# One TensorE order, two build-time plans: what a matmul is charged, and a new table by slot

## The chip, the cores and the metric

The kernel runs on one core of one Trainium2 chip. The metric is the device time of one launch in microseconds (us). Three runs of the kernel before gave 1040.53, 1040.58 and 1040.61 us; the median is 1040.58 us.

## The reference

Two attention branches, A and B, read the same `x` (2048 tokens by 640) with their own weights; a sigmoid gate by token mixes their outputs. Each branch has 32 heads of width 20, and works through the tokens in 4 segments of 512:

```python
for s in range(N):                       # 4 segments, for each branch
    qs, ks, vs = q[:, :, s], k[:, :, s], v[:, :, s]
    logits = einsum("bhqd,bhkd->bhqk", qs, ks) * scale + mask     # causal within the segment
    a_dot = einsum("bhqk,bhkd->bhqd", softmax(logits), vs)
    num = einsum("bhld,bhde->bhle", phi(qs), M); den = phi(qs) . z + 1e-6
    outs.append(g * num / den + (1 - g) * a_dot)                  # g by head
    M, z = M + phi(ks)^T vs, z + sum(phi(ks))
o = outs @ wo
result = gate * o_A + (1 - gate) * o_B
```

## The kernel before, in words

The work is cut into 8 blocks (branch and segment), and each block into 8 quads of four heads: 64 quads, and 66 **slots** `i` in which they are worked through. For each quad there are S units (the logits with queries on partitions, whose row maxima VectorE takes, line 1058), one transpose of the maxima (`mrow_unit`, line 1096), T units (the logits again with keys on partitions, the maxima in two extra rows; ScalarE's exp at line 1153 and GpSimd's causal select at line 1154 make `p`), and a PV unit (`pv_unit`, line 1181: 16 fp32 matmuls with 128 rows and 32 columns each, 32 rows in the profile, since an fp32 matmul runs in two passes). Around these lie the products with wq, wk, wv, wo, each split into three terms of hi and lo parts (`product`, line 640, 512 or 320 columns wide), the reads and updates of the memory `M` (`mem_unit`, line 749, and `update_unit`, line 827, fp32 in two passes), and transposes (`turn`, line 787).

Almost every matmul uses 64 of the 128 rows of TensorE: an instruction goes to the lower or to the upper **half**, and one of each half can run side by side. PV, the first two products (line 685) and the last (line 1000) use all rows, so both halves must come to an end before them.

The order of the instructions on every engine is made **while the kernel is built**, by a planner written in the kernel itself. It keeps a clock `now`, a time `lane[half]` at which each half of TensorE is free, and a queue for each other engine with a pace for each of its instructions (`put("D", 0.63, ...)`: VectorE for 0.63 us; A is ScalarE, G GpSimd, S the DMA queue), and `DONE`, the delay until another engine sees the end. `step` picks the half that is free first, and `lane_step` takes for it, in this order, an S or T matmul, the second half of a unit whose first half is done (`seconds`), or the first half of a new unit (`firsts`). What is emitted stands in TensorE's program in this order, and TensorE takes its matmuls in the order of the program. The chip sees only the order and the semaphores: the planner's paces and clocks aren't in the program.

`RULES` is a table by slot: the order of the ten S and T units, and five numbers (`span`, `calm`, `lag`, `room`, `hold`) that say how the slot is spread over the products, when work for VectorE is held back, how long after the first half the second may follow, how many buffers must be free, and by how much the slot begins early. A slot without an entry keeps the entry of the slot before.

The charges of TensorE's instructions before:

```python
STEP, STEPV = 0.2335, 0.1475                      # a product of 512, of 320 columns
(w * 0.000458, ...)                               # S and T, w columns
(0.063, ...)                                      # a transpose
max(0.22, (c - a) * E1 * 0.0017)                  # a memory read;   update: nh * E1 * 0.0017
now[0] = max(now[0], lane[0], lane[1]) + 0.09     # PV; then w * 0.00174 for each kb, and 0.063
```

Of the kernel before, what the change touches and what calls it, by code (L numbers as in the profile page):

```python
# [16 lines left out]
ALU = mybir.AluOpType  # L17

P = 128
# [23 lines left out]
def tile_gated_mix_infini_attn(  # L43
# [47 lines left out]
        0: "STSTSTSTST 1.010 2.38 0.36 8 0.0",  # L91
        1: "TSTSTSTSTS 1.010 2.19 0.30 8 0.0",
        3: "TSTSTSTSTS 1.010 2.38 0.30 8 0.0",
        4: "TSTSTSTSTS 1.010 2.38 0.32 6 0.0",
        5: "TTSSTTSSTS 1.010 2.38 0.30 8 0.0",
        6: "TSTSTSTSTS 1.010 2.38 0.30 8 0.0",
        8: "TSTSTSTSTS 1.045 2.38 0.30 4 0.0",
        9: "TSTSTSTSTS 1.010 2.38 0.35 8 0.0",
        10: "TSTSTSTSTS 1.021 2.38 0.32 8 0.0",
        12: "TSTSTSTSTS 1.010 2.38 0.30 8 0.0",  # L100
        14: "TSTSTSTSTS 0.957 2.38 0.37 6 0.0",
        15: "TSTSTSTSTS 0.932 2.30 0.32 8 0.0",
        16: "TSTSTSTSTS 1.010 2.38 0.30 8 0.0",
        19: "TSTSTSTSTS 1.002 2.63 0.30 8 0.0",
        21: "TSTSTSTSTS 1.010 2.51 0.30 4 0.0",
        22: "TSTSTSTSTS 0.927 1.90 0.30 4 0.0",
        23: "TTSTSTSTSS 1.012 2.26 0.37 8 0.0",
        24: "TSTSTSTSTS 1.010 2.38 0.30 8 0.0",
        25: "TSTSTSTSTS 1.010 3.35 0.30 8 0.0",
        27: "TSTSTSTSTS 1.010 2.38 0.30 8 0.0",  # L110
        28: "TSTSTSTSTS 0.939 3.03 0.35 8 0.0",
        30: "TSTSTSTSTS 1.010 2.38 0.30 8 0.0",
        32: "TTSTSTSTSS 1.010 2.38 0.30 8 0.0",
        34: "TSTSTSTSTS 1.010 2.38 0.30 8 0.0",
        36: "TSTSTSTSTS 1.040 2.50 0.30 6 0.0",
        37: "TSTSTSTSTS 0.950 2.38 0.30 6 0.0",
        39: "TSSTTSSTTS 1.010 1.60 0.37 8 0.0",
        41: "TSSTTSSTTS 1.010 2.38 0.33 6 0.0",
        42: "TSTSTSTSTS 0.939 2.38 0.30 4 0.0",
        46: "TSTSTSTSTS 1.010 2.38 0.30 8 0.0",  # L120
        49: "TSTSTSTSTS 1.010 2.38 0.25 4 0.0",
        50: "TSTSTSTSTS 1.010 2.38 0.30 8 0.0",
        54: "TSSTTSSTTS 1.019 3.32 0.30 6 0.0",
        57: "TSTSTSTSTS 1.010 2.38 0.30 8 0.0",
        58: "TSTSTSTSTS 1.014 3.04 0.30 8 0.0",
        60: "TSTSTSTSTS 1.010 2.38 0.30 8 0.0",
        61: "STSTSTSTST 1.047 2.95 0.38 8 6.0",
        62: "TSTSTSTSTS 1.010 2.38 0.30 8 0.0",
        63: "TSTSTSTSTS 1.014 2.38 0.25 4 0.0",
        64: "TSTSTSTSTS 1.010 2.38 0.30 8 0.0",  # L130
    }
    rule = {}
    DONE = {"A": 0.165, "D": 0.11, "G": 0.1, "S": 0.0}
# [69 lines left out]

    def whole(dur, emit):
        now[0] = max(now[0], lane[0], lane[1]) + dur
        got = emit()
        lane[:] = [now[0], now[0]]
        advance(now[0])
        return got
# [160 lines left out]
    STEP, STEPV = 0.2335, 0.1475  # L370

# [47 lines left out]
    def stage(i):  # L419
# [8 lines left out]
        lo_cost = 0.9 if i < 4 else 1.6  # L428
        if kind == "v":
# [6 lines left out]
            def piece(w, a, b, wh, wl, done):  # L436
                n = b - a
                w3 = w.rearrange("p (k n) -> p k n", n=VN)[:, :n, :]

                def landed():  # L440
                    put("A", 0.33 * n, lambda: nc.scalar.copy(wh[:, a:b, :], w3), split_lo, prio=6)

                def split_lo():
                    put("G", 0.8 * n, lambda: nc.gpsimd.tensor_tensor(
                        out=wl[:, a:b, :], in0=w3, in1=r32(wh[:, a:b, :]), op=ALU.subtract), end, prio=4)
# [10 lines left out]
        def got(w):  # L456
# [8 lines left out]
            def split_hi(pair):  # L465
                wh, wl = pair
                put("A", 0.66, lambda: nc.scalar.copy(wh, w3), lambda: put(  # L467
# [15 lines left out]
    def want_x(s, k):  # L483

        def got(hi, lo, st):
            def landed():
                put("A", 0.56, lambda: nc.scalar.copy(hi, r32(st)), low, prio=6)

            def low():
                e, eng, cost = ("D", nc.vector, 0.7) if s == 0 else ("G", nc.gpsimd, 1.3)  # L490
# [91 lines left out]
    def hi_lo_phi(pp, hi, lo, y, dst, m, then, got_phi):  # L582
# [7 lines left out]
        if load["D"] < load["A"]:  # L590
            def over():
                put("D", 0.63, lambda: nc.vector.tensor_scalar(pp, pp, 0.0, 1.0, op0=ALU.max, op1=ALU.add), lambda: put(  # L592
                    "D", 0.63, lambda: nc.vector.tensor_tensor(out=r32(y), in0=pp, in1=r32(y), op=ALU.min), end, prio=1), prio=1)  # L593
# [3 lines left out]
            put("A", 0.49, lambda: nc.scalar.activation(r32(y), pp, AF.Exp), read, prio=1)  # L597
        else:
            both = then_all(2, lambda: put("D", 0.63, lambda: nc.vector.scalar_tensor_tensor(
                out=r32(y), in0=pp, scalar=0.0, in1=r32(y), op0=ALU.max, op1=ALU.add), end, prio=1))  # L600
            hi_lo_out(pp, hi, lo, dst, m, both, then)
            put("A", 0.49, lambda: nc.scalar.activation(r32(y), pp, AF.Relu, scale=-1.0), lambda: put(  # L602
                "A", 0.56, lambda: nc.scalar.activation(r32(y), r32(y), AF.Exp, scale=-1.0), both, prio=1), prio=1)

    def hi_lo_out(src, hi, lo, dst, m, read, then):
        is_q = any(dst is x for x in qd)

        def low():
            put("D", 0.63, lambda: nc.vector.tensor_tensor(out=lo, in0=src, in1=r32(hi), op=ALU.subtract), out, prio=1)  # L609
# [15 lines left out]
        put("A", 0.49, lambda: nc.scalar.copy(hi, src), low, prio=1)  # L625
# [11 lines left out]
    def product(bank_of, terms, step, done):  # L637
        def mm(half, n, start, stop):
# [3 lines left out]
        ops = [[(step, lambda a, z, half=half, n=n: mm(half, n, a, z)) for n in range(len(terms))] for half in range(2)]  # L642
# [86 lines left out]
    def mem_unit(t, n, h):  # L729
# [17 lines left out]
        def mm(half, j, start, stop):  # L747
# [8 lines left out]
        ops = [[(max(0.22, (c - a) * E1 * 0.0017), lambda z0, z1, half=half, j=j: mm(half, j, z0, z1)) for j, (m, a, c) in enumerate(pieces[half])]  # L756
# [24 lines left out]
        return split_unit(*ops, lambda: (read(), put("D", 1.05, weigh, end, prio=4)))  # L781

    def turn(px, block):
# [5 lines left out]
        return [[(0.063, lambda a, z, half=half, n=n: one(half, n)) for n in range(NB)] for half in range(2)]  # L789
# [4 lines left out]
    def back_unit(t, m, pk):  # L794
# [3 lines left out]
        def got(pkn):  # L798
# [4 lines left out]
            either(0.52, lambda: nc.scalar.copy(r32(pkn), b), 0.63, lambda: nc.vector.tensor_copy(r32(pkn), b), end, 3)  # L803
# [16 lines left out]
    def update_unit(t, m, pkn):  # L820
# [5 lines left out]
        def mm(half, n, start, stop):  # L826
# [6 lines left out]
        ops = [[(nh * E1 * 0.0017, lambda a, z, half=half, n=n: mm(half, n, a, z)) for n in range(NB)] for half in range(2)]  # L833
# [5 lines left out]
        def take():  # L839
            big.give(pkn)  # L840
            if s == 0:
                put("D", 0.3, lambda: nc.vector.tensor_copy(mbd[m], v), lambda: (
                    bank.give(b), put("G", 0.8, lambda: keep_own_heads(mbd[m], m), end, prio=2)), prio=3)
            else:
                def got(tmp):
                    def add():
# [3 lines left out]
                    put("D", 0.3, lambda: nc.vector.tensor_copy(tmp[:, :nh, :], v), lambda: (  # L850
                        bank.give(b), put("G", 1.4, add, lambda: (mt_store.give(tmp), end()), prio=2)), prio=3)
# [5 lines left out]
    def job_v(t, half):  # L857
# [9 lines left out]
        for n in range(NB):  # L867
# [7 lines left out]
            def take(pp=pp, n=n):  # L875
                through()
                put("A", 0.37, lambda: nc.scalar.copy(
# [10 lines left out]
    def job_o(t, m):  # L888
# [32 lines left out]
        def got(ot):  # L921
# [8 lines left out]
            def take():  # L930
                if b == 0:
                    put("A", 0.49, lambda: nc.scalar.copy(r32(ot), pp), send, prio=2)  # L932
                elif pt:
                    put("D", 0.63, lambda: nc.vector.tensor_tensor(
# [10 lines left out]
    def job_early(t, m):  # L945
# [21 lines left out]
        def take():  # L967
# [3 lines left out]
            put("D", 0.63, lambda: nc.vector.tensor_tensor(  # L971
# [4 lines left out]
    def job_last(t):  # L976
# [4 lines left out]
        def finish(m):  # L981
# [3 lines left out]
            put("D", 0.63, lambda: nc.vector.tensor_tensor(  # L985
# [54 lines left out]
    def s_unit(i, n):  # L1040
# [5 lines left out]
        for half in range(2):  # L1046
# [3 lines left out]
            def look(half=half, sc=sc):  # L1050
# [5 lines left out]
                def one(pair, qb, off, then):  # L1056
                    w = P * (qb + 1)
                    put("D", w / 960.0 + 0.112, lambda: nc.vector.tensor_tensor_reduce(  # L1058
# [10 lines left out]
            for j, (pair, qb, off) in enumerate(todo):  # L1069
                w = P * (qb + 1)  # L1070
                lane_ops[half].append((w * 0.000458, lambda pair=pair, qb=qb, off=off, w=w, r=r, sc=sc: nc.tensor.matmul(  # L1071
# [5 lines left out]
    def m_unit(i):  # L1077
# [4 lines left out]
        put("A", 0.2, lambda: nc.scalar.copy(mt[:, :, 0, :], m), lambda: put(  # L1082
            "G", 0.25, lambda: nc.gpsimd.tensor_tensor(
# [7 lines left out]
    def mrow_unit(i):  # L1091
# [4 lines left out]
        ops = [[(0.063, lambda a, z, r=r: nc.tensor.transpose(b[:32, r], mtf[r], ident[r, r]))] for r in ROWS]  # L1096

        def got(mr):
# [14 lines left out]
            put("A", 0.26, lambda: nc.scalar.copy(mr, b[:32, :P]), send, prio=1)  # L1113
# [16 lines left out]
    def t_unit(i, n):  # L1130
# [10 lines left out]
        for half in range(2):  # L1141
# [6 lines left out]
            def take(half=half, sc=sc, pt=pt, blocks=blocks):  # L1148
                def finished():
# [3 lines left out]
                put("A", 0.49, lambda: nc.scalar.activation(pt, sc, AF.Exp, scale=SCALE), lambda: (bank.give(sc), put(  # L1153
                    "G", 0.08 + 0.16 * len(todo), lambda: nc.gpsimd.affine_select(  # L1154
# [4 lines left out]
            for j, (pair, kb, off) in enumerate(todo):  # L1159
                w = L - P * kb  # L1160
                lane_ops[half].append((w * 0.000458, lambda pair=pair, kb=kb, off=off, w=w, r=r, sc=sc: nc.tensor.matmul(  # L1161
# [7 lines left out]
    def pv_unit(i):  # L1169
# [3 lines left out]
        now[0] = max(now[0], lane[0], lane[1]) + 0.09  # L1173
        advance(now[0])
        for kb in range(NB):
# [24 lines left out]
        def got(oT):  # L1200
# [5 lines left out]
            either(0.52, lambda: nc.scalar.copy(r32(oT), po), 0.63, lambda: nc.vector.tensor_copy(r32(oT), po), end, 2)  # L1206
# [17 lines left out]
    def fin_unit(i):  # L1224
# [24 lines left out]
        def take():  # L1249
            big.give(oT)  # L1250
            if s == 0:
                put("D", 0.95, lambda: weigh(o), lambda: (bank.give(b), end()), prio=2)
            else:
                def got(tmp):
                    e, eng, cost = ("D", nc.vector, 0.45) if i >= 62 else ("G", nc.gpsimd, 0.9)
                    put("D", 0.95, lambda: weigh(tmp), lambda: (bank.give(b), put(
# [9 lines left out]
    def o_transpose(t, k):  # L1266
# [3 lines left out]
        def got(hi, lo):  # L1270
# [4 lines left out]
            put("A", 0.49, lambda: nc.scalar.copy(hi, b), lambda: put("D", 0.63, lambda: nc.vector.tensor_tensor(  # L1275
# [69 lines left out]
    def lane_step(half):  # L1345
# [7 lines left out]
        if u and max(now[0], lane[half]) >= u["at"]:  # L1353
# [51 lines left out]
    def wait(what):  # L1405
# [6 lines left out]
        now[0] = max(now[0], clk[0])  # L1412
# [124 lines left out]
```

## Time and profile before

| what | value |
|---|---|
| median of three runs | 1040.58 us |
| profiled execution: span on the core | 1038.6 us, 31967 instructions |
| its own time beside the span | only the span is given for this execution; the median lies 2.0 us above it |
| TensorE busy / its weight loads | 1031.3 us (99%) / 874.8 us (84%) |
| VectorE, ScalarE, GpSimd busy | 765.4 us (74%), 661.7 us (64%), 581.7 us (56%) |
| DMA queue q1 | 205.93 MB, 65.7% of 16 engines |

"Busy" counts a matmul from its start to its modelled end, and matmuls overlap: a 512-wide one stands at 404 ns in the table of groups, while a half takes one in a good half of that. So 99% doesn't say that TensorE couldn't be quicker; the distance from one start to the next does. In the timeline a row "x10" is ten like instructions with nothing else between them on the engine, with the start of the first and the time to the end of the last.

### The profile page before, as it was taken

How to read it: one execution, taken by the hardware profiler on the slowest of the kernel's cores; microseconds unless marked ns; L12 is line 12 of the kernel's file. 1: busy time of each engine (PE TensorE's matmuls, PEld its weight loads, DVE VectorE, ACT ScalarE, POOL GpSimd, SP SyncE). 2: the span in 40 equal slices, each digit the busy share in tenths (PEclk: the TensorE clock that was granted, in tenths of full speed). 3: DMA queues.
4: the chain of work that ended last, by engine and by line, in shares of the span. 5: the costliest groups of instructions: out<-in, count | busy, mean ns of one | idle time of the engine just before them, and what ended most of it. 6: DMA issues, size and time to landing. Idle time of an engine off the chain costs nothing.

```text
span 1038.6 us, 31967 instructions
## 1 busy us (share of the span) xinstructions
PE 1031.3 (99%) x11780; PEld 874.8 (84%) x11780; DVE 765.4 (74%) x2726; ACT 661.7 (64%) x1336; POOL 581.7 (56%) x1043
## 2 busy tenths in 40 slices
PE   9999999999999999999999999999999999999998
PEld 7988888898888879898888978989879888888876
DVE  4687787579686788676886868865787867778764
ACT  6367666578565585666756567665676656657681
POOL 4465555566454564666645557555674537636471
PEclk9999999999999999999999999999999999999999
DMA  8996767478466686755855568675585865847531
GB/s 275 290 290 201 224 195 230 132 225 271 143 194 187 181 272 175 241 150 158 261 171 190 172 176 290 194 211 174 161 253 157 266 167 181 273 125 244 140 120 51
DMA packets 110028, 207.97 MB, mean 200 GB/s; under 512 B 12464, under 2 KB 16560, under 8 KB 109872
## 3 DMA queue, kind: packets, MB, share of 16 engines
q1 hardware_dynamic: 109872, 205.93, 65.7%
q8 instruction: 93, 1.52, 0.6%
q14 instruction: 63, 0.52, 0.2%
HBM read 131.43 MB, written 73.40 MB: 197 GB/s over the span
## 4 chain that ended last, share of the span: by engine, by line
PE 92%; DVE 1%; ACT 0%; issue 0%; ACTq 0%; DVEq 0%
PE bank L640 53%; PE bank L1181 14%; PE bank L1071 7%; PE bank L1161 7%; PE bank L787 4%; PE bank L749 3%; PE bank L827 3%; PE bank L1096 1%; PE bank L1000 0%; DVE row L985 0%; ACT p L1153 0%; DVE bank L1058 0%; DVE row L593 0%; ACT row L932 0%; DVE bank L592 0%
## 5 line engine op out<-in xcount | busy, mean ns | idle before, releaser
L1058 DVE CUSTOM_DVE_ANT_0 bank<-bank,tri 128x128 f32<-128x128 f32 (+3 forms) x1024 | 475.1, 518 | 157.4 <-PE bank L1071 126.0
L640 PE MATMUL bank<-row,wh 64*128 64x512 f32 x2308 | 525.7, 404 | 0.0
L1153 ACT ACTIVATE p<-bank 128x512 f32<-128x512 f32 x592 | 326.5, 599 | 141.6 <-PE bank L1161 112.8
L1154 POOL TENSOR_SCALAR_AFFINE_SELECT p<-p 128x256 f32<-128x256 f32 (+1 forms) x592 | 213.9, 369 | 268.5 <-ACT p L1153 252.1
L640 PEld LDWEIGHTS bank<-row,wh 64*128 64x128 f32 x2308 | 326.1, 185 | 11.8 <-issue 1.8
L640 PE MATMUL bank<-row,wl 64*128 64x512 f32 x1154 | 310.3, 402 | 0.0
L469 POOL TENSOR_TENSOR wl<-wst,wh 128x640 fp32r<-128x640 f32 x115 | 179.6, 1565 | 72.0 <-ACT wh L467 71.5
L640 PE MATMUL bank<-wvh,row 64*128 64x320 f32 x1280 | 189.8, 316 | 0.0
L640 PEld LDWEIGHTS bank<-row,wl 64*128 64x128 f32 x1154 | 175.0, 185 | 5.6 <-issue 0.6
L1161 PE MATMUL bank<-qst,kst 62*128 62x128 f32 (+3 forms) x1024 | 173.5, 319 | 0.0
L1071 PE MATMUL bank<-kst,qst 60*128 60x128 f32 (+3 forms) x1024 | 171.7, 320 | 0.2
L640 PEld LDWEIGHTS bank<-wvh,row 64*128 64x128 f32 x1280 | 154.1, 185 | 3.9 <-issue 2.0
L1181 PE MATMUL bank<-p,vst 128*32 128x384 f32 (+3 forms) x1932 | 146.0, 430 | 0.0
L1058 DVE DVE_READ_ACCUMULATOR2_ANT mx<- 128x1 f32 x1024 | 143.3, 140 | 0.0
L1071 PEld LDWEIGHTS bank<-kst,qst 60*128 60x128 f32 x1024 | 123.7, 185 | 12.0 <-issue 2.5
L1161 PEld LDWEIGHTS bank<-qst,kst 62*128 62x128 f32 x1024 | 124.9, 185 | 7.5 <-issue 1.2
L1181 PEld LDWEIGHTS bank<-p,vst 128*32 128x32 f32 x1932 | 58.3, 109 | 85.7 <-issue 61.4
L640 PE MATMUL bank<-wvl,row 64*128 64x320 f32 x640 | 109.4, 312 | 0.0
L467 ACT CAST wh<-wst 128x640 fp32r<-128x640 f32 x119 | 86.2, 735 | 30.8 <-PE bank L640 15.5
L640 PEld LDWEIGHTS bank<-wvl,row 64*128 64x128 f32 x640 | 85.0, 185 | 0.5 <-issue 0.2
L609 DVE TENSOR_TENSOR row<-bank,row 128x512 fp32r<-128x512 f32 x80 | 54.9, 688 | 38.3 <-ACT row L602 18.4
L1206 ACT COPY row<-bank 128x512 f32<-128x512 f32 x60 | 35.2, 587 | 70.7 <-PE bank L1181 68.8
(100 smaller groups left out, 1289.9 us busy)
## 6 DMA issues: line engine op xcount, KB each, us to landing
qd<-row SPq DMA_DIRECT2D x120, 256.0 KB
kd<-row SPq DMA_DIRECT2D x120, 256.0 KB
qst<-qd SPq DMA_DIRECT2D x128, 240.0 KB
kst<-kd SPq DMA_DIRECT2D x128, 240.0 KB
wst<-in_a_wq_dram SPq DMA_DIRECT2D x20, 320.0 KB
wst<-in_a_wk_dram SPq DMA_DIRECT2D x20, 320.0 KB
wst<-in_b_wq_dram SPq DMA_DIRECT2D x20, 320.0 KB
wst<-in_b_wk_dram SPq DMA_DIRECT2D x20, 320.0 KB
```

The source lines that it names most:

```text
L467: put("A", 0.66, lambda: nc.scalar.copy(wh, w3), lambda: put(lo_eng, lo_cost, lambda: lo.tensor_tensor(out=wl, in0=w3, in1=r32(wh), op=ALU ...
L469: lambda: lo.tensor_tensor(out=wl, in0=w3, in1=r32(wh), op=ALU.subtract), end, prio=3), prio=6)
L609: put("D", 0.63, lambda: nc.vector.tensor_tensor(out=lo, in0=src, in1=r32(hi), op=ALU.subtract), out, prio=1)
L640: return nc.tensor.matmul(bank_of, lhsT=w[ROWS[half]], rhs=x_[ROWS[half]], start=start, stop=stop)
L787: return nc.tensor.transpose(px[:, n, r], block(n)[r], ident[r, r])
L1058: put("D", w / 960.0 + 0.112, lambda: nc.vector.tensor_tensor_reduce(out=sc[:, off:off + w], in0=sc[:, off:off + w], in1=tri[:, L - w:], s ...
L1071: lane_ops[half].append((w * 0.000458, lambda pair=pair, qb=qb, off=off, w=w, r=r, sc=sc: nc.tensor.matmul(sc[:, off:off + w], lhsT=q[r, p ...
L1153: put("A", 0.49, lambda: nc.scalar.activation(pt, sc, AF.Exp, scale=SCALE), lambda: (bank.give(sc), put("G", 0.08 + 0.16 * len(todo), lamb ...
L1154: "G", 0.08 + 0.16 * len(todo), lambda: nc.gpsimd.affine_select(out=blocks, in_=blocks, pattern=[[0, len(todo)], [1, P]], base=0, channel_ ...
L1161: lane_ops[half].append((w * 0.000458, lambda pair=pair, kb=kb, off=off, w=w, r=r, sc=sc: nc.tensor.matmul(sc[:, off:off + w], lhsT=k[r, p ...
L1181: nc.tensor.matmul(po[32 * j:32 * j + 32, P * kb:], lhsT=vst[t % 2][:, kb, h * E1:h * E1 + 32], rhs=pts[i, n, f][0][:, off:off + w], start ...
L1206: either(0.52, lambda: nc.scalar.copy(r32(oT), po), 0.63, lambda: nc.vector.tensor_copy(r32(oT), po), end, 2)
```

## The change

The set of instructions on TensorE stays the same, and so do their shapes. What changes is what the planner charges, hence the order, and the table.

1. A matmul on a half has a form now: the time it streams, a lead by which its weights must have been fetched before it starts, and a number of parts (two for fp32). A fetch begins at the earliest 0.003 us after the matmul ahead on the same half has begun, and 0.03 us after the last fetch of either half. A short matmul thus holds its half for 0.116 us, until the next one's weights are there.
2. PV and the whole-array products wait for a fetch of their own; PV has an entry of 0.109 us and an exit of 0.11 us.
3. The paces of the other engines are set anew, most of them by a few per cent (0.63 to 0.605, 0.49 to 0.483, 1.6 to 1.52), `DONE` a little longer.
4. `RULES` has an entry for each of the 66 slots, most of them new.

```diff
-    DONE = {"A": 0.165, "D": 0.11, "G": 0.1, "S": 0.0}
+    DONE = {"A": 0.17, "D": 0.135, "G": 0.11, "S": 0.0}
+    FULL, LEADT = 0.113, 0.056
+    def mm(n):
+        return 0.008 + n * 0.0004333, FULL, 1
+    def quad4(n):
+        return 0.0027 + n / 1200.0, FULL, 2
+    TURN = (0.029, LEADT, 1)
...
+    def next_start(half, lead):
+        fetch = max(begun[half] + 0.003, fetched[0] + 0.03)
+        return fetch, max(now[0], lane[half], fetch + lead)
-    def op(half, dur, emit):
+    def op(half, form, emit):
+        stream, lead, parts = form
+        joined[0] = False
+        fetched[0], start = next_start(half, lead)
         now[0] = max(now[0], lane[half])
+        for _ in range(parts - 1):
+            start += max(stream, 0.003 + lead)
+        begun[half], lane[half] = start, start + stream
         advance(now[0])
-        got = emit()
-        lane[half] = now[0] + dur
-        return got
+        return emit()
...
-        ops = [[(step, lambda a, z, half=half, n=n: mm(half, n, a, z)) ...
+        form = PROD if step == STEP else PRODV        # mm(L), mm(VN)
+        ops = [[(form, lambda a, z, half=half, n=n: run(half, n, a, z)) ...
-        ops = [[(max(0.22, (c - a) * E1 * 0.0017), ...
+        ops = [[(quad4((c - a) * E1), ...
-                lane_ops[half].append((w * 0.000458, ...
+                lane_ops[half].append((mm(w), ...
...
-        now[0] = max(now[0], lane[0], lane[1]) + 0.09
+        now[0] = max(now[0], lane[0], lane[1]) + 0.109
-            now[0] += w * 0.00174
+            now[0] += 2 * (w / 1200.0 + 0.0027)
-        now[0] += 0.063
-        lane[:] = [now[0], now[0]]
+        now[0] += 0.11
+        lane[:] = begun[:] = [now[0], now[0]]
+        fetched[0] = now[0]
...
-        if u and max(now[0], lane[half]) >= u["at"]:
+        if u and next_start(half, u["ops"][half][0][0][1])[1] >= u["at"]:
...
-        0: "STSTSTSTST 1.010 2.38 0.36 8 0.0",      # RULES: 40 entries before
-        1: "TSTSTSTSTS 1.010 2.19 0.30 8 0.0",
+        0: "TTSTSTSTSS 1.055 2.80 0.30 8 0.0",      # 66 entries after
+        1: "TSSTTSSTTS 1.010 2.38 0.33 4 0.0",
+        2: "STTSTSSTST 1.010 1.93 0.39 8 0.0",
```

More of the change, by code (lines that the diff above doesn't have):

```diff
@@ L202, in tile_gated_mix_infini_attn @@
     seconds = [deque(), deque()]
+    begun = [0.0, 0.0]
+    fetched = [0.0]
+    joined = [True]
     def whole(dur, emit):
-        now[0] = max(now[0], lane[0], lane[1]) + dur
+        if not joined[0]:
+            lane[:] = [max(now[0], *lane) + 0.1] * 2
+            begun[:] = lane
+            joined[0] = True
+        fetched[0] = max(max(begun) + 0.003, fetched[0] + 0.03)
+        start = max(now[0], lane[0], lane[1], fetched[0] + FULL)
+        begun[:] = [start, start]
+        now[0] = start + dur
         got = emit()
@@ L637, in product, with run @@
     def product(bank_of, terms, step, done):
-        def mm(half, n, start, stop):
+        def run(half, n, start, stop):
             w, x_ = terms[n]()
             return nc.tensor.matmul(bank_of, lhsT=w[ROWS[half]], rhs=x_[ROWS[half]], start=start, stop=stop)
-        ops = [[(step, lambda a, z, half=half, n=n: mm(half, n, a, z)) for n in range(len(terms))] for half in range(2)]
+        form = PROD if step == STEP else PRODV
+        ops = [[(form, lambda a, z, half=half, n=n: run(half, n, a, z)) for n in range(len(terms))] for half in range(2)]
         yield split_unit(*ops, done, step / 2)
@@ L745, in mem_unit, with run @@
                     pieces[half].append((m, a, c))
-        def mm(half, j, start, stop):
+        def run(half, j, start, stop):
             m, a, c = pieces[half][j]
@@ L787, in one @@
             return nc.tensor.transpose(px[:, n, r], block(n)[r], ident[r, r])
-        return [[(0.063, lambda a, z, half=half, n=n: one(half, n)) for n in range(NB)] for half in range(2)]
+        return [[(TURN, lambda a, z, half=half, n=n: one(half, n)) for n in range(NB)] for half in range(2)]
     def got_pk(t, m, pk):
@@ L824, in update_unit, with run @@
         b = bank.free.pop(0)
-        def mm(half, n, start, stop):
+        def run(half, n, start, stop):
             return nc.tensor.matmul(
@@ L831, in mm @@
             )
-        ops = [[(nh * E1 * 0.0017, lambda a, z, half=half, n=n: mm(half, n, a, z)) for n in range(NB)] for half in range(2)]
+        ops = [[(quad4(nh * E1), lambda a, z, half=half, n=n: run(half, n, a, z)) for n in range(NB)] for half in range(2)]
         v = b[:, :nh * E1].rearrange("p (h e) -> p h e", e=E1)
@@ L1070, in s_unit @@
                 w = P * (qb + 1)
[L1071 removed]
+                lane_ops[half].append((mm(w), lambda pair=pair, qb=qb, off=off, w=w, r=r, sc=sc: nc.tensor.matmul(
                     sc[:, off:off + w], lhsT=q[r, pair, P * qb:P * (qb + 1)], rhs=k[r, pair, 0:w], start=True, stop=True,
@@ L1095, in mrow_unit @@
         mtf = r32(mt.rearrange("p f c n -> p (f c n)"))
-        ops = [[(0.063, lambda a, z, r=r: nc.tensor.transpose(b[:32, r], mtf[r], ident[r, r]))] for r in ROWS]
+        ops = [[(TURN, lambda a, z, r=r: nc.tensor.transpose(b[:32, r], mtf[r], ident[r, r]))] for r in ROWS]
         def got(mr):
@@ L1160, in t_unit @@
                 w = L - P * kb
-                lane_ops[half].append((w * 0.000458, lambda pair=pair, kb=kb, off=off, w=w, r=r, sc=sc: nc.tensor.matmul(
+                lane_ops[half].append((mm(w), lambda pair=pair, kb=kb, off=off, w=w, r=r, sc=sc: nc.tensor.matmul(
                     sc[:, off:off + w], lhsT=k[r, pair, P * kb:P * (kb + 1)], rhs=q[r, pair, P * kb:],
```

163 lines of the change are left out of this document (95 added, 68 removed).

## The prediction

> **What bounds the kernel now.** I read the profile's page first, then TensorE's waits, then the windows.
>
> ```profile
> span 1038.6 us, 31967 instructions
> ...
> PE 1031.3 (99%) x11780; PEld 874.8 (84%) x11780; DVE 765.4 (74%) x2726; ACT 661.7 (64%) x1336; POOL 581.7 (56%) x1043
> ...
> PE 92%; DVE 1%; ACT 0%; issue 0%; ACTq 0%; DVEq 0%
> ```
>
> ```profile
> PE bank L281 <- DVE qst L285: 1.5, 1, 1.5
> PE bank L1096 <- ACT p L1153: 0.7, 1, 0.7
> ```
>
> ```profile
> 0.00:62.00 62.00, 60.37 (x544) 53.41 (x548) 38.58 (x126) 34.60 (x66) 30.28 (x48) 1.00 0.89 280
> 62.00:541.00 479.00, 478.70 (x5621) 406.81 (x5623) 364.21 (x1300) 316.13 (x643) 272.95 (x493) 1.00 0.68 205
> 541.00:1020.40 479.40, 478.66 (x5535) 403.96 (x5531) 354.70 (x1288) 309.21 (x626) 278.50 (x504) 1.00 0.64 190
> 1020.40:1038.60 18.20, 13.59 (x90) 10.60 (x90) 7.93 (x14) 1.76 (x3) 0.00 (x0) 0.93 0.21 72
> ```
>
> The reader is to see that the chain that ended last is TensorE (PE) for 92%, that PE waits 2.2 us in all for other engines, and that the clock is 1.00 until the tail. So the time is made of how closely PE's matmuls follow one another. "Busy" can't show that, since matmuls overlap. I take paces from rows of the timeline where like instructions stand together and both halves are at work (start to start; where a row stands alone, its time less one matmul, over the count less one):
>
> ```profile
> 14.62 1.44 PE L640 MATMUL bank<-row,wh 64*128 64x512 f32 x10
> 15.89 1.31 PE L640 MATMUL bank<-row,wl 64*128 64x512 f32 x10
> 17.04 1.31 PE L640 MATMUL bank<-row,wh 64*128 64x512 f32 x10
> 18.18 0.40 PE L787 MATMUL bank<-ident,row 64*128 64x64 f32 x4
> ...
> 435.77 1.84 PE L640 MATMUL bank<-wvh,row 64*128 64x320 f32 x21
> 437.32 1.03 PE L640 MATMUL bank<-wvl,row 64*128 64x320 f32 x10
> 438.06 1.04 PE L640 MATMUL bank<-wvh,row 64*128 64x320 f32 x11
> ...
> 510.70 0.41 PE L1071 MATMUL bank<-kst,qst 60*128 60x384 f32 x4
> 510.94 0.90 PE L640 MATMUL bank<-row,wh 64*128 64x512 f32 x5
> 511.46 0.84 PE L640 MATMUL bank<-row,wl 64*128 64x512 f32 x4
> 511.93 0.49 PE L1161 MATMUL bank<-qst,kst 62*128 62x256 f32 x3
> ...
> 317.12 0.49 PE L1161 MATMUL bank<-qst,kst 62*128 62x256 f32 x4
> 317.36 0.39 PE L640 MATMUL bank<-row,wh 64*128 64x512 f32 x1
> ...
> 97.14 0.48 PE L827 MATMUL bank<-vst,row 64*128 64x147 f32 x4
> 258.91 1.94 PE L749 MATMUL bank<-mbd,row 64*128 64x84 f32 x26
> ```
>
> ```profile
> 1018.08 2.29 PE bank L1181 x32
> ```
>
> A 512-wide matmul costs 1.15 / 10 = 0.115 us (15.89 to 17.04), so 0.23 on its half; a 320-wide one 2.29 / 31 = 0.074 (435.77 to 438.06); a 256-wide one 0.24 / 4 = 0.06; a transpose about 0.06 on its half, 0.03 with both at work; an update pass 0.062, a memory pass 0.067; a PV unit 2.29 (the last row, from the chain). Four S matmuls, two 384 and two 128 wide, are followed 0.24 us later by products; but the half that goes to line 1161 at 511.93 ran four products since 510.94 in 0.99 us, where 4 x 0.23 = 0.92: some 0.06 is paid behind the 128-wide one, so the four cost 0.30, or 0.075 each.
>
> With the counts of the build: 14.6 (until 14.62) + 3480 x 0.115 + 1920 x 0.074 + S and T (512 x 0.115 + 1024 x 0.075 + 512 x 0.06) + 64 x 2.29 + 1200 x 0.03 + 480 x 0.062 + 528 x 0.067 + 30 whole-array products x 0.23 + 4.6 at the end (18.20 - 13.59) = 982.6 us. The span is 1038.6. So about **56 us** go where one half stands still. One place of this kind, in the timeline:
>
> ```profile
> 264.67 0.47 PE L1071 MATMUL bank<-kst,qst 60*128 60x384 f32 x4
> 264.98 1.51 PE L640 MATMUL bank<-wvh,row 64*128 64x320 f32 x13
> ```
>
> Thirteen 320-wide products take (1.51 - 0.30) / 12 = 0.10 each, with 0.074 possible: by the program's order the first six all go to the upper half, and the lower one, done with its 128-wide matmul, gets its next behind them.
>
> **The change, part by part.** *Work.* TensorE has 10252 matmul instructions in both builds, of like shapes; DMAs are as many; VectorE, ScalarE and GpSimd differ in a dozen evacuations that go to the other engine. At 0.6 to 0.7 us each that is below 10 us on engines that have over 270 us to spare: nothing on the path.
>
> *The order of the halves* is where the change can act. I count in both programs each turn in which one half gets instruction after instruction: since PE starts matmuls in order, the other half's next can't start before the turn's last. The turn's sum without its last, by the paces above per half (0.23, 0.148, 0.19 for 384 and 0.12 for 128, 0.12 for 256 and for the memory, 0.126 for updates, 0.06), less the other half's last instruction, is time in which that half must stand still; halved, since only half the array does. For 264.98 the turn begins with the upper half's own 128-wide matmul: 0.12 + 5 x 0.148 - 0.12 = 0.74, halved 0.37.
>
> Before: 241 such turns, 22.7 us. After: 158 turns, 8.7 us. The long ones go: of more than 0.3 us, 51 (11.9 us) become 6 (1.5); of 0.15 to 0.3 us, 55 (5.9) become 28 (3.1); the small ones stay, 135 (5.0) and 124 (4.1). That is **-14.0 us**.
>
> A second working goes over all pairs of neighbours: for each pair of forms, on the same half or on the other, the mean distance of their ends in the trace (11780 rows, the first and the last of them below), times the pairs of the new order. It gives **-15.9 us** for the stretch between the first and the last PV. With two preceding instructions instead of one it gives -18.5, and that made from every other stretch between PVs alone -11 or -22. It sees more than turns: a half that is served with shorter matmuls than the other loses too. I take -16.
>
> ```profile
> 1.51 4.08 PE L281 MATMUL bank<-qst 128*128 128x512 f32 x9 [1.51 <-DVE qst L285]
> ...
> 1033.68 0.40 PE L1000 MATMUL bank<-row,wvh 128*128 128x512 f32 x1
> ```
>
> *PV's entry and exit, waits, head and tail.* There are 64 PV units in both; the pair table puts their entries at within 0.2 us of before in sum. The new paces of the other engines only move when the planner thinks data is there. Its cover is the distance in PE's own stream: from a quad's last T matmul to its PV it was at least 1.16 us, 2.53 in the median, and becomes 1.70 and 2.67; from the last S matmul to the maxima's transpose 4.78 in the median becomes 4.22; from there to the first T matmul 10.9 becomes 12.2. I take nothing, with 2.2 us (the waits of before) as the most that could be gained. The first PV comes some 17 matmuls earlier, the work lying behind it instead; the tail is the same code. Nothing for either.
>
> *A rule against the change.* The change charges a matmul for the load of its successor's weights. The trace has that at 0.06 us behind a 128-wide matmul (row 511.93) and at nothing behind a 512-wide one (0.23 per half, steadily). The Trainium skill (TensorE: Matmul & The Clock Gate, Step-by-step: what each phase is for) says that TensorE pulls the next weights' load ahead of matmuls in flight, so that it runs beside them; read without a limit, the charge would be for nothing. The trace agrees only where the matmul ahead is long.
>
> *Sum.* 1038.6 - 16 = 1022.6 for the span; the median of the runs lies 2.0 above the profiled span, so **1024.6 us**.
>
> **The rivals.**
> *Only part comes back* (1032 to 1038.5): a turn taken away can leave the half waiting a little later, for PV stops both halves 64 times anyway. Against it: the pair table holds such sequels as far as the old order has them. The low end of its halves, -11, is near this case.
> *The load is hidden after all*, by the rule above: then each of the 512 128-wide matmuls holds its half for 0.058 instead of 0.116 us, and the planner hands the other half work for 0.058 us in which this one stands still: 512 x 0.058 / 2 = 15 us lost again, 1039.6 us: no change. The 0.06 in row 511.93 speaks against it.
> *Slower: PV meets its data.* PV's first matmul waits for the quad's last `p`, and all of PE's program is queued behind it. If PV comes one select too early, each waits that long:
>
> ```profile
> L1154 POOL TENSOR_SCALAR_AFFINE_SELECT p<-p 128x256 f32<-128x256 f32 x374 | 150.4, 412 | 114.8 <-ACT p L1153 106.3
> ```
>
> 64 x 0.412 = 26.4 us, and 1024.6 + 26.4 = 1051 us. It decides from 18.1 / 26.4, 44 of 64 PVs, on (16 of the gain and 0.2% of the time, 2.1). For it: new paces are mostly shorter, so the planner trusts the engines more. Against it: the shortest distance from T to PV grows from 1.16 to 1.70 us.
> *More than forecast* (below 1017): the planner's picture of the halves fits the chip wherever the old order has no like place; the longest contexts point there.
>
> **How the numbers follow.** 0.2% (2.1 us) is about what a measurement of this kernel can tell from no change. Forecast, 1017 to 1032 us: 0.65; only part: 0.14; more: 0.08; no change: 0.04; slower: 0.09. Faster 0.65 + 0.14 + 0.08 = 0.87. The range takes the forecast's bounds (-11 and -22 give 1029.6 and 1018.6), and reaches up into the partial case to 1036 and down by the waits and the longer contexts to 1013; some 0.03 lie below and 0.15 above.
>
> **What would show it.** After the change, the page should again have PE at 99% and VectorE's share up by about one point; PE's waits should stay below 4 us in all; PV units should stay at 2.29 us; the count and the busy time of products should be the same, and the windows between PVs shorter all along, by about 0.25 us per slot (16 / 64). Rows such as 264.98, many products of one line at 0.10 instead of 0.074, should be rarer. It is wrong if PE's waits, or what stands idle before line 1181, grow by more than 10 us, or if the span falls by less than 8 us with the waits unchanged: then turns were not what cost the time.

## The result, and the profile after

The changed kernel took **1043.73 us** (median of 5 runs, 1042.96 to 1045.06), the kernel before 1040.53 on the same chip (5 runs, 1039.93 to 1040.61): a ratio of 1.0028 with a 95% interval of 1.0015 to 1.0041. It is slower by 3.2 us, where 16 us less had been forecast. The profiled execution took 1042.96 us, with a span of 1041.3.

The page after, with the rows that answer to those of before:

```profile
span 1041.3 us, 31917 instructions
...
PE 1031.3 (99%) x11780; PEld 870.4 (84%) x11780; DVE 760.8 (73%) x2725; ACT 660.2 (63%) x1337; POOL 581.7 (56%) x1043
...
PE 89%; DVE 3%; DMA 3%; ACT 2%; issue 1%; POOL 1%; SPq 0%; ACTq 0%; DVEq 0%; POOLq 0%
```

The work on every engine is nearly what it was. In the chain that ended last PE's share falls from 92% to 89%, and VectorE's rises from 1% to 3%, with DMA and ScalarE beside it. This is a hint that other engines now decide at some places when PE goes on, and no more than a hint: the shares of before add up to 93% only, and table_margin, a quicker kernel further down, has PE at 78%.

TensorE's own waits hardly show it: they come to 4.2 us, 2.2 before. While a matmul is held, the one ahead of it still stands as "busy" for a part of that time (in the last two rows of the timeline below PE idles for 0.33 us and its weight loads for 0.59 us, at one and the same wait), so one must ask the weight loads (PEld). The loads of the T matmuls (line 1161 before, 1217 after), before and then after; the idle time ahead of the loads stands behind the second bar:

```profile
L1161 PEld LDWEIGHTS bank<-qst,kst 62*128 62x128 f32 x1024 | 124.9, 185 | 7.5 <-issue 1.2 <-DVE mx L1058 1.0 <-DVE row L593 0.3
```
```profile
L1217 PEld LDWEIGHTS bank<-qst,kst 62*128 62x128 f32 x1024 | 125.3, 185 | 17.1 <-DVE mx L1114 4.6 <-DVE row L648 2.4 <-DVE mw L819 1.2
```

7.5 us become 17.1, and of what the rows name, VectorE's part grows from 1.3 to 8.2. The same from the other side: who waited for the row maxima (line 1058 before), us and times, before and after:

```profile
  ACT mt L1082: 31.3, 28
  ACT p L1153: 2.5, 2
  PEld bank L1181: 2.2, 7
  PEld bank L1071: 1.3, 6
  PEld bank L1161: 1.0, 4
```
```profile
  ACT mt L1138: 38.0, 31
  ACT p L1209: 8.4, 5
  PEld bank L1217: 4.6, 20
  PEld bank L1127: 2.9, 12
  PEld bank L1237: 0.7, 2
```

S and T matmuls (lines 1127 and 1217 after) write into a bank of PSUM that VectorE has just read; 10 such waits of 2.3 us before became 32 of 7.5 us. One of them in the timeline after:

```profile
657.87 1.12 PE L695 MATMUL bank<-wvh,row 64*128 64x320 f32 x12
657.97 0.14 DVE L1114 DVE_READ_ACCUMULATOR2_ANT mx<- 128x1 f32 x1
657.97 0.47 DVE L1114 CUSTOM_DVE_ANT_0 bank<-bank,tri 128x256 f32<-128x256 f32 x1
...
658.36 0.47 DVE L1114 CUSTOM_DVE_ANT_0 bank<-bank,tri 128x256 f32<-128x256 f32 x1
...
658.74 0.47 DVE L1114 CUSTOM_DVE_ANT_0 bank<-bank,tri 128x256 f32<-128x256 f32 x1
...
659.12 0.17 DVE L819 SCALAR_TENSOR_TENSOR mw<-bank,gqm 128x19 f32<-128x19 f32 x1
659.32 0.30 PEld L1217 LDWEIGHTS bank<-qst,kst 62*128 62x128 f32 x4 [0.59 <-DVE mw L819]
659.32 0.50 PE L1217 MATMUL bank<-qst,kst 62*128 62x384 f32 x4 [0.33 <-DVE mw L819]
```

VectorE works without a pause; its 256-wide row maxima start 0.385 us apart. The new pace of the planner says 256 / 960 + 0.085 = 0.352; the old one, with 0.112, said 0.379. The T matmuls behind line 819 stand where the planner thought VectorE would be; PE is through its products, and its weight loads idle for 0.59 us.

I measure this for every run in one way: from the semaphores' events I take for each matmul the last release by another instruction. In every trace the distances from release to start pile up at 0.043 to 0.045 us: I take the matmuls that sit there as held by that release. The time by which each starts later than its half and the instruction ahead allow is its standing still. For releases by VectorE: 60 matmuls, 3.8 us before; **121 matmuls, 12.6 us** after. Turns (one half served again and again, counted in the order as in the prediction) and these waits:

| kernel | us | turns counted | waits for VectorE |
|---|---|---|---|
| before | 1040.5 | 22.7 | 3.8 (60) |
| after | 1043.7 | 8.7 | 12.6 (121) |
| after_matched | 1037.7 | 8.7 | 7.4 (77) |
| after_narrow | 1032.2 | 8.7 | 4.2 (33) |
| before_narrow | 1036.8 | 22.7 | 1.9 (23) |
| before_extra | 1040.7 | 22.7 | 4.0 (67) |
| before_one_rule | 1084.2 | 49.1 | 7.2 (85) |
| charges_one_rule | 1064.9 | 27.9 | 8.8 (101) |
| after_one_rule | 1075.7 | 31.5 | 11.8 (117) |
| after_dve085 | 1088.0 | 31.0 | 12.8 (110) |
| table_right_pace | 1039.1 | 9.6 | 4.7 (63) |
| table_margin | 1034.3 | 11.1 | 3.5 (46) |
| table_margin_2 | 1032.3 | 9.7 | 4.1 (39) |
| table_more_margin | 1037.6 | 11.5 | 2.9 (28) |

### The profile page after: what moved, and what is told of

The parts are those of the page before. It is cut to its first block, busy times and chain, and to the rows that moved or that the text cites. A ratio compares the mean times of both kernels' runs of the same rounds, so it can differ in the third digit from the quotient of the medians.

```text
span 1041.3 us, 31917 instructions
## 1 busy us (share of the span) xinstructions
PE 1031.3 (99%) x11780; PEld 870.4 (84%) x11780; DVE 760.8 (73%) x2725; ACT 660.2 (63%) x1337; POOL 581.7 (56%) x1043
## 3 DMA queue, kind: packets, MB, share of 16 engines
q8 instruction: 93, 1.52, 0.6%
## 4 chain that ended last, share of the span: by engine, by line
PE 89%; DVE 3%; DMA 3%; ACT 2%; issue 1%; POOL 1%; SPq 0%; ACTq 0%; DVEq 0%; POOLq 0%
PE bank L695 52%; PE bank L1237 13%; PE bank L1217 7%; PE bank L1127 7%; PE bank L843 4%; PE bank L883 3%; PE bank L805 2%; DVE bank L1114 1%; DMA kd<-row 1%; DMA wst<-in_x_dram 1%; PE bank L741 1%; PE bank L1152 0%; POOL wl L524 0%; DMA row<-in_xT_dram 0%; PE bank L1056 0%
## 5 line engine op out<-in xcount | busy, mean ns | idle before, releaser
L1114 DVE CUSTOM_DVE_ANT_0 bank<-bank,tri 128x384 f32<-128x384 f32 (+3 forms) x1024 | 474.0, 522 | 146.3 <-PE bank L1127 117.6
L695 PE MATMUL bank<-row,wh 64*128 64x512 f32 x2308 | 535.2, 407 | 0.0
L1209 ACT ACTIVATE p<-bank 128x512 f32<-128x512 f32 x606 | 333.3, 599 | 155.6 <-PE bank L1217 124.5
L695 PE MATMUL bank<-row,wl 64*128 64x512 f32 x1154 | 302.5, 402 | 0.0
L695 PE MATMUL bank<-wvh,row 64*128 64x320 f32 x1280 | 202.4, 317 | 0.1
L1127 PE MATMUL bank<-kst,qst 60*128 60x384 f32 (+3 forms) x1024 | 176.9, 321 | 0.9 <-DVE O L1304 0.4
L1217 PE MATMUL bank<-qst,kst 62*128 62x384 f32 (+3 forms) x1024 | 172.8, 323 | 1.1 <-DVE mw L819 0.7
L695 PEld LDWEIGHTS bank<-wvh,row 64*128 64x128 f32 x1280 | 161.1, 185 | 2.9 <-issue 1.4
L1237 PE MATMUL bank<-p,vst 128*32 128x128 f32 (+2 forms) x1980 | 148.3, 430 | 0.0
L1217 PEld LDWEIGHTS bank<-qst,kst 62*128 62x128 f32 x1024 | 125.3, 185 | 17.1 <-DVE mx L1114 4.6
L499 POOL TENSOR_TENSOR wvl<-wst,wvh 128x640 fp32r<-128x640 f32 (+1 forms) x48 | 63.9, 1336 | 21.3 <-ACT wvh L496 21.0
```

Source lines behind the costliest of these rows:

```text
L499: put("G", 0.77 * n, lambda: nc.gpsimd.tensor_tensor(out=wl[:, a:b, :], in0=w3, in1=r32(wh[:, a:b, :]), op=ALU.subtract), end, prio=4)
L695: return nc.tensor.matmul(bank_of, lhsT=w[ROWS[half]], rhs=x_[ROWS[half]], start=start, stop=stop)
L1114: put("D", w / 960.0 + 0.085, lambda: nc.vector.tensor_tensor_reduce(out=sc[:, off:off + w], in0=sc[:, off:off + w], in1=tri[:, L - w:], s ...
L1127: lane_ops[half].append((mm(w), lambda pair=pair, qb=qb, off=off, w=w, r=r, sc=sc: nc.tensor.matmul(sc[:, off:off + w], lhsT=q[r, pair, P ...
L1209: put("A", 0.483, lambda: nc.scalar.activation(pt, sc, AF.Exp, scale=SCALE), lambda: (bank.give(sc), put("G", 0.15 + 0.105 * len(todo), la ...
L1217: lane_ops[half].append((mm(w), lambda pair=pair, kb=kb, off=off, w=w, r=r, sc=sc: nc.tensor.matmul(sc[:, off:off + w], lhsT=k[r, pair, P ...
```

## The experiments

The kernel before, run beside them, had medians of 1040.4 to 1040.9 us.

**VectorE quicker, with each plan and all orders as they are** (two kernels, the same edit in both; the planner's pace stays what it was; exp's scale is lowered as well, not shown):

```diff
-                    w = P * (qb + 1)
+                    w, c = P * (qb + 1), min(P * (qb + 1), 256 - P * (qb < 2))
-                        out=sc[:, off:off + w], in0=sc[:, off:off + w], in1=tri[:, L - w:],
+                        out=sc[:, off + w - c:off + w], in0=sc[:, off + w - c:off + w], in1=tri[:, L - c:],
```

after_narrow: 

> The changed kernel with the same plan and the same order on every engine, but VectorE's row maxima read 128, 128, 256 and 256 columns instead of 128, 256, 384 and 512 (part of the maximum is left out, and exp's scale is reduced so that nothing overflows). VectorE has some 137 us less to do, 4 x 512 columns / 960 per us for each of 64 quads. Theory 1 (PE waits for VectorE: in the trace after, PE starts 121 matmuls 0.044 us after a release by VectorE, 12.6 us of standing still, against 60 and 3.8 before, because the new paces are 0.027 us too short per row maximum and PE's charges no longer leave a cushion): 1043.7 - 12 = about 1031 us, and those late starts nearly gone. Rival (the releases only coincide; the new order itself is no better): 1041 to 1044.

before_narrow: 

> The kernel before with the same shortened row maxima. Theory 1: only 3.8 us of waiting for VectorE to take away, so 1037 to 1038 us; the distance between this and after_narrow is then what the order of the halves is worth, 6 to 14 us. Rival: 1039 to 1041, no distance between the two.

Measured: 1032.21 us (ratio to before 0.9921, 0.9905 to 0.9938) and 1036.83 (0.9961, 0.9947 to 0.9975). The kernel after gains 11.5 us, the one before 3.7. In the trace of after_narrow, of those who waited for the row maxima:

```profile
  PEld bank L1237: 1.1, 3
  PEld bank L1217: 0.5, 2
  PEld bank L1127: 0.5, 1
```

VectorE's busy time falls by 123 us (760.8 to 637.8) and by 125 us. Its lateness, with all that hangs on it, costs the changed kernel about 11 us, and with VectorE out of the way the new order is ahead by 4.6 us: below the 6 that I had put as its least.

**VectorE quicker by about what the new pace is short**, and **a small instruction more on VectorE** in the kernel before, meant to make it slower than the old plan believes; orders untouched:

```diff
 after_matched
-                    w = P * (qb + 1)
+                    w, c = P * (qb + 1), P * (qb + 1) - 35 * (qb > 0)
 before_extra
-                    put("D", w / 960.0 + 0.112, lambda: nc.vector.tensor_tensor_reduce(
+                    put("D", w / 960.0 + 0.112, lambda: (half or nc.vector.memset(scrap, 0.0), nc.vector.tensor_tensor_reduce(
```

after_matched: 

> The changed kernel with its plan and orders untouched, and VectorE made as quick on the chip as the new pace believes: three of four row maxima read 35 columns less (35 / 960 = 0.036 us, 0.027 us per row maximum on average; part of the maximum is left out, exp's scale reduced). If the pace that is 0.027 us too short is what makes VectorE late: most of the 8.8 us of added waiting goes, 1043.7 - 8 = about 1035 us, against 1032.2 with VectorE much quicker. If it is the lost cushion on TensorE's side instead, with paces a side matter: 1039 to 1042.

before_extra: 

> The kernel before, same plan and orders, and VectorE made slower than its plan believes: a one-column memset ahead of every second row maximum, 512 x about 0.06 = 31 us, the size by which the new pace errs (1024 x 0.027 = 28). If the old plan has a cushion against it (its charges for TensorE are too low, so PE runs behind the plan): below 1043. If the error of the pace costs the same here as after the change: 1040.7 + 9 = about 1049. If VectorE's lateness is no cause at all: 1040 to 1041.

Measured: 1037.74 us (0.9970, 0.9960 to 0.9981) and 1040.71 (0.9998, 0.9989 to 1.0007). The first removes 6.0 us; the row maxima's waiters stand between those of after and of after_narrow:

```profile
  PEld bank L1217: 2.5, 8
  PEld bank L1127: 1.2, 5
```

The second adds 512 small instructions and costs nothing at all:

```profile
L1059 DVE MEMSET scrap<- x512: 59/59/59, 30.7 to 1001.2; 128x1 f32 x171
```
```profile
  PEld bank L1182: 2.5, 8
  PEld bank L1072: 1.4, 7
  PEld bank L1162: 1.2, 5
```

Their records come to 512 x 0.059 = 30 us, but VectorE was not made slower by that: its busy time rises by 2.4 us only, from 765.4 to 767.8. A like run of 256-wide row maxima, before and in before_extra:

```profile
55.18 0.43 DVE L1058 CUSTOM_DVE_ANT_0 bank<-bank,tri 128x256 f32<-128x256 f32 x1 [0.30 <-PE bank L1071]
...
55.53 0.47 DVE L1058 CUSTOM_DVE_ANT_0 bank<-bank,tri 128x256 f32<-128x256 f32 x1
...
55.91 0.46 DVE L1058 CUSTOM_DVE_ANT_0 bank<-bank,tri 128x256 f32<-128x256 f32 x1
...
56.29 0.47 DVE L1058 CUSTOM_DVE_ANT_0 bank<-bank,tri 128x256 f32<-128x256 f32 x1
```
```profile
55.13 0.43 DVE L1059 CUSTOM_DVE_ANT_0 bank<-bank,tri 128x256 f32<-128x256 f32 x1 [0.29 <-PE bank L1072]
...
55.49 0.46 DVE L1059 CUSTOM_DVE_ANT_0 bank<-bank,tri 128x256 f32<-128x256 f32 x1
55.56 0.06 DVE L1059 MEMSET scrap<- 128x1 f32 x1
...
55.86 0.46 DVE L1059 CUSTOM_DVE_ANT_0 bank<-bank,tri 128x256 f32<-128x256 f32 x1
...
56.25 0.46 DVE L1059 CUSTOM_DVE_ANT_0 bank<-bank,tri 128x256 f32<-128x256 f32 x1
```

The memset begins beside the row maximum that is under way (55.56, inside 55.49 + 0.46). From the first to the fourth row maximum it is 1.11 us without the memset and 1.12 us with it. So before_extra says nothing of whether the old plan could bear a slower VectorE.

The rows of before show a second thing: the first row maximum of a run has 0.35 us until the next, each later one 0.38. That holds at all widths. For 128, 256, 384 and 512 columns one that follows another directly has 0.249, 0.382, 0.515 and 0.649 us (medians), which is 0.03 more than the new pace says (0.218, 0.352, 0.485, 0.618); the first of a run has 0.206, 0.350, 0.483 and 0.616, as the new pace says or a little less. In the trace after, 708 of the 1024 follow another directly, so the pace is short by about 708 x 0.03 = 21 us in all (an estimate). after_matched took more than that away: 768 x 0.036 = 28 us by its edit, 24.9 us by VectorE's busy time (760.8 to 735.9). So the error of this one pace is at most about half of the 11.5 us.

**What the parts do with one rule for all slots.** Here the table is one entry, so that it is fitted to none of the cost sets. charges_one_rule is the kernel before with the new charges of TensorE put in as well; after_one_rule has the new paces on top:

```diff
     RULES = {
+        0: "TSTSTSTSTS 1.010 2.38 0.30 8 0.0",      # nothing else
     }
```

before_one_rule: 

> The kernel before with a table of one entry, TSTSTSTSTS 1.010 2.38 0.30 8 0.0, for all 66 slots. The turns in its order come to 49.1 us of one half standing still (22.7 before). If counted turns cost their time: 1040.5 + 26.4 = about 1067 us. If turns cost nothing (the rival to the prediction's main step): 1040 to 1045.

charges_one_rule: 

> The new charges of TensorE alone (weight load, PV entry and exit), the old paces of the other engines, and the same table of one entry. Its turns come to 27.9 us. If turns cost their time: 1040.5 + 5.2 = about 1046 us, some 21 below before_one_rule, so that the charges by themselves make a better plan. If they cost nothing: the two within 5 us of each other. Waits for VectorE should stay below 6 us, since the paces are the old ones.

after_one_rule: 

> New charges and new paces, with the table of one entry. Turns 31.5 us, against 27.9 in charges_one_rule (new charges, old paces; 1064.9 us). If the new paces make VectorE late here too: 1064.9 + 3.6 + 5 to 9 = 1073 to 1078. If the paces are harmless by themselves: 1065 to 1069.

Measured: 1084.15 us (1.0426, 1.0368 to 1.0484), 1064.87 (1.0232, 1.0215 to 1.0249) and 1075.74 (1.0343, 1.0309 to 1.0377). The new charges alone are worth 19.3 us by the medians, where they take away 21.2 us of turns (49.1 to 27.9). A part of the 19.3 is TensorE's clock: the four runs of before_one_rule took 1078.3, 1081.7, 1086.6 and 1093.1 us at granted clocks of 0.998, 0.996, 0.990 and 0.985, those of charges_one_rule 1063.1 to 1066.2 at 0.998 to 1.000. In the profiled run the clock stands at half for 7 us, behind a stretch in which 320-wide products start 0.15 us apart, those of one half alone:

```profile
744.30:751.20 6.90, 6.42 (x41) 5.96 (x41) 5.57 (x20) 3.72 (x8) 1.68 (x3) 0.51 0.90 317
```

Between the runs at 0.998 (one and two) it is 13 to 14 us, less than the turns' 21.2. The new paces on top cost 10.9 us, with 3.6 us of turns and 3.0 us of waits for VectorE more; the rest isn't placed. Both absolute forecasts for the first two were 17 to 19 us too low: an unfitted table brings more than turns.

**One number put back in the changed kernel:**

```diff
-                    put("D", w / 960.0 + 0.085, lambda: nc.vector.tensor_tensor_reduce(
+                    put("D", w / 960.0 + 0.112, lambda: nc.vector.tensor_tensor_reduce(
```

after_dve085: 

> The changed kernel with one number put back: 0.112 instead of 0.085 in the pace of a row maximum, which is what the trace has (0.617 to 0.649 us for 512 columns). The planner makes a whole new order of it, with the table found for the other number: its turns come to 31.0 us instead of 8.7. If the table fits only the costs that it was made with: 1043.7 + 22 - 9 = about 1057 us. If a right pace is what counts: 1033 to 1036.

Measured: 1088.04 us (1.0456, 1.0433 to 1.0479), 31 more than the nearer forecast. The table fits the costs that it was made with and no others; with a number nearer to the trace in it the planner gives another order altogether. Its turns are 22.3 us more, its clock was 0.991 to 0.995, and its weight loads wait longer for GpSimd (3.8 us before PV, 2.0 in the trace after); for VectorE matmuls wait about as long (12.8 us, 12.6 after):

```profile
PEld bank L1237 <- POOL p L1210: 3.8, 10, 1.3
PEld bank L1217 <- DVE mx L1114: 3.6, 8, 1.4
PEld bank L1127 <- DVE ft L1304: 3.1, 5, 1.4
PEld bank L1237 <- DVE mx L1114: 2.5, 8, 0.4
```

A part undone thus tells nothing of the part unless the table is made anew.

**Right paces, tables made anew.** Four kernels with the new charges, VectorE's paces nearer to the trace (0.112 for every row maximum), and a table searched slot by slot against the planner's own clock (66 entries each, not shown). They differ in a margin on VectorE:

```diff
-    DONE = {"A": 0.17, "D": 0.135, "G": 0.11, "S": 0.0}
+    DONE = {"A": 0.17, "D": 0.165, "G": 0.11, "S": 0.0}          # table_margin, table_margin_2
-                    put("D", w / 960.0 + 0.085, ...
+                    put("D", w / 960.0 + 0.142, ...              # 0.112 and 0.030 of margin
-                put("D", 0.9, lambda: weigh(o), ...
+                put("D", 0.97, lambda: weigh(o), ...
```

table_right_pace (no margin): 

> The changed kernel's charges with the traced paces of VectorE (a row maximum at w / 960 + 0.112, the division after PV at 0.97) and a table searched anew for these costs, from one rule, slot by slot, against the planner's own clock. Its turns come to 9.6 us. If a right pace and a table made for it are what counts: about what after_matched has, 1036 to 1039 us, with waits for VectorE at 5 to 8 us instead of 12.6. If every other order of this kind scatters by tens of us, as after_dve085's did: above 1045.

table_margin: 

> The same, with a margin on VectorE on top: 0.030 us more for a row maximum, and 0.030 us more until its end is seen; table searched for these costs. Turns 11.1 us. If the cushion is what kept the kernel before from waiting for VectorE (before_extra): waits for VectorE below 5 us and 1031 to 1036 us, faster than both kernels in spite of 1.5 us more of turns. If a margin only makes the plan longer: 1037 to 1041.

table_margin_2: 

> The same costs as table_margin (0.030 us of margin on VectorE), with a table from a longer search. Turns 9.7 us, against 11.1. If turns and waits for VectorE go on counting as they did: 1034.3 - 1.4 = about 1033 us, waits for VectorE below 5 us. If orders of one and the same cost set scatter by more than that: 1029 to 1039.

table_more_margin (0.060): 

> The margin doubled: 0.060 us more for a row maximum and until its end is seen; table searched for these costs with the same length of search. Turns 11.5 us. If there is still waiting for VectorE to be taken away: 1031 to 1034, waits for VectorE below 3 us. If 0.030 was enough and the rest only makes the plan longer: 1034 to 1038.

Measured: 1039.13 us (0.9987, 0.9977 to 0.9996), **1034.27** (0.9937, 0.9918 to 0.9956), **1032.33** (0.9918, 0.9901 to 0.9936) and 1037.60 (0.9972, 0.9963 to 0.9981). table_margin_2 computes the whole result and is 8.2 us quicker than the kernel before. Its page, and its waiters for the row maxima:

```profile
span 1030.5 us, 31946 instructions
...
PE 1021.8 (99%) x11780; PEld 876.8 (85%) x11780; DVE 761.3 (74%) x2720; ACT 661.4 (64%) x1342; POOL 580.7 (56%) x1043
```
```profile
  PEld bank L1237: 2.2, 7
  PEld bank L1127: 0.7, 3
  PEld bank L695: 0.5, 1
  PEld bank L1217: 0.2, 1
```

The waits of the S and T matmuls for the row maxima were 4.6 and 2.9 us after the change. The right pace with its own table has 1.0 and 1.1; the margin takes away what is left (0.2 and 0.7 here, 0.5 and none in table_margin). Waits for VectorE in all fall by about 1 us from table_right_pace to the two tables with the margin (4.7 to 3.5 and 4.1), and turns don't fall, so most of the 4.9 and 6.8 us between them isn't explained by either. Double the margin takes no more away that would count and is slower; its waits for ScalarE (5.2 us by the same measure, 0.9 in table_margin_2) are no sign of the margin, since table_margin has about as many. Two tables for one and the same cost set lie 1.9 us apart, and each other cost set has one table only: what a margin is worth by itself is not shown.

## Why the prediction was wrong

*The bound* was right: PE's order sets the time in both.

*The turns* went the way that was forecast. In the two traces, between the first and the last PV, halves stand still in the counted turns for 18.0 us before and 5.9 after: -12.1, against -14.0. The size hangs on the count: with each half's end carried on through the program, the same traces give 14.7 and 5.8, so -8.9.

*"I take nothing" for the waits* is the step that failed. It rested on a cover, the distance from T to PV, that is not where PE waits: it waits at S and T matmuls for a bank that VectorE must have read. And it took the new paces for a detail, although the rows of before price them: held against the distances above, the new pace would have been seen to be 0.03 us short wherever one row maximum follows another, 677 times in the trace of before. What it cost: waits for VectorE rose by 8.8 us, and taking VectorE out of the way was worth 11.5 us after the change and 3.7 before it, so 7.8 us of the 19.2 between forecast and result.

*A cushion in the old plan* may be why the same VectorE was less late there; no run shows it, since before_extra didn't slow VectorE and no kernel has the old charges with the new paces. What can be read is how far PE falls behind each plan. From the first PV to the last the planner's clock has 921.4 us before, 940.5 after and 939.2 in table_margin_2; the traces have 956.1, 960.3 and 947.3. So PE ends 34.7, 19.8 and 8.1 us late, and every other engine had that much more time than planned. The old plan charged a 128-wide matmul 0.059 us instead of 0.116 (PV comes to 2.38 and 2.37 us in the two plans), and VectorE's 512-wide passes 0.63 us where they start 0.60 to 0.61 apart. That table_margin_2, with the least lag, waits little for VectorE fits a margin taking the cushion's place; it is an argument.

*The sum of the order's worth* was mis-sized as well. With VectorE quick in both, the new order is 4.6 us ahead, not 14 to 16. By the paces of the prediction the loss between the first and the last PV is 54.8 us before and 56.5 after (51.4 and 45.5 in the narrow pair). The turns' -12.1 and VectorE's +8.8 leave 5 us that came elsewhere (2 us with -8.9 for the turns). In the narrow pair, by the first count, 6 us are missing, of which 2.3 are VectorE's rest (1.9 to 4.2 in the table). Where the remainder lies, perhaps in loads that can't be fetched ahead behind a held matmul, was not tried, and stays open. The pair table, which priced places by the old order alone, could not see any of it.

*The rivals.* "Slower" came true by its kind, PE meeting its data, at another place and a third of the price. The load "hidden after all" did not: the charges alone gave 13 to 19 us with one rule, and the trace of before has the load. Behind a 128-wide matmul and a 512-wide product on one half, the next product comes 0.285 us after the first (median of 267), against 0.232 among products alone. The sign by which it was to be seen wrong, a span that falls by less than 8 us with PE's waits unchanged, is nearly what the page shows (the span rose by 2.7 us, the waits by 2.0); but the conclusion tied to it, that turns were not what cost the time, went too far: fewer turns did bring 4.6 us in the narrow pair, and the waits stood in the rows of the weight loads.

## What to carry to other kernels

A plan made at build time is only as good as its worst cost, and its errors may shelter one another (argued here, not shown): before one side's costs are made true, hold every other pace against the start-to-start distances in the trace, runs and single instructions apart. Before a run that adds work to an engine is used as proof, see in its trace that the engine did become slower. A table searched against one set of costs belongs to that set; change one number and it must be made again before the change is judged. When an engine shows no waits but the time grows, ask its weight loads and its chain of waits, not its busy time.

## What the runs showed of the hardware

A matmul held by a semaphore starts 0.043 to 0.045 us after the release; in every trace the distances pile up there. A row maximum of w columns from PSUM that directly follows another has about w / 960 + 0.115 us until the next instruction of VectorE (0.249, 0.382, 0.515 and 0.649 for 128 to 512 columns), the first of a run 0.03 to 0.04 us less (0.206, 0.350, 0.483, 0.616); the read of the accumulator lies within. A one-column memset between two row maxima has a record of 0.059 us and doesn't make the run longer (1.12 us against 1.11 for four). TensorE's granted clock fell to half in the middle of two runs, for 7 us in before_one_rule (0.51) and for 14 us in after_dve085 (0.50).
